# Fewer attention bursts hand part of their exponentials to VectorE: 52 instead of 76, with other scratch space

## The chip, the cores and the metric

The kernel runs on one NeuronCore of a Trainium2 chip. The core has TensorE (PE, matrix products), ScalarE (ACT, activation functions), VectorE (DVE, elementwise work and scans), GpSimd (POOL) and SyncE (SP, which here issues nearly all DMAs). The engines run side by side and wait for each other through semaphores. The metric is the time of one execution on the device in microseconds (us). A difference of 0.2% (1.9 us) is about what a measurement of this kernel can tell from no change.

## The reference

The input x is one sequence of 2048 tokens by 1024 features. Two branches work on it and a gate mixes them:

```
g = sigmoid((x * gate_w).sum(-1))
a = S5(x)          # diagonal complex state-space model, 1024 states
b = MHA(x)         # 32 heads of 32, no mask
out = g * a + (1 - g) * b

# S5:   Bu = x @ B_bar^T ; h_t = Lam_bar * h_(t-1) + Bu_t ; y = 2 Re(C h) + x * Dskip
# MHA:  q,k,v = x @ wqkv ; p = softmax(q k^T / sqrt(32)) ; o = (p v) @ wo
```

The softmax needs 32 x 2048 x 2048 exponentials. They are the largest single piece of work outside TensorE.

## The kernel before, in words

**Bursts.** The 32 heads are worked in 8 groups of four heads (g = 0 to 7), each group in 8 units of 256 queries, each unit in 8 bursts of 256 keys: 512 bursts, numbered B, and p is the same number as a place in time. One burst computes the scores of 4 heads x 256 keys x 256 queries (`burst`, L1651: 8 matmuls on 32 rows each) into two score slots of PSUM out of three, z = 0 and z = 1; a slot holds 128 x 1024 numbers. `exp` (L1658) turns a slot into bf16 weights in SBUF, normally by one ScalarE instruction of 1024 columns per slot (L1667). So a normal burst costs ScalarE two such instructions. `pv` (L1725) later multiplies the weights into V, four small matmuls to a "quarter" and four quarters to a burst; `plan` deals the quarters out over later bursts.

**Shared bursts.** For the bursts in the set `DVB`, `dve_exp` splits slot z = 0: ScalarE does only the first half of it (512 columns, L1692), and VectorE does the other half by integer arithmetic in five instructions: L1693 from PSUM, then L1698 to L1701 (`exp_b` to `exp_f`). I call these bursts shared. They stand at most at every fourth place (B % 4 == 1), so a stretch of four bursts holds one half and seven full exponentials, or eight full ones. The five VectorE instructions need scratch: two result tiles (`xt`), an integer tile (`xi`) and a float tile (`xw`). `x_set` says which of five places a burst uses: the projection weights' buffer `w` of one or the other parity (with the second half of `Ag`), the upper half of the state buffer `hp`, rows 6 and 7 of `OT`, or `ut` and `ub`. Each place belongs to something else at other times, and `x_toks` puts the dependences on whatever writes there next.

**Dense work.** Between the bursts TensorE works off chains of large matmuls ("dense" work), all through PSUM bank 7: projections for the next group (`d_qk` L1422, `d_v` L1440), the state inputs u (`d_u` L1452), the state outputs c (`d_c`: 16 matmuls L1481 and 4 small ones L1487 for the skip term), and at the end the output projection (`d_out` L1512). A chain is 8 large matmuls (c: 16; V: 32 small ones), and VectorE copies its result out of bank 7 before the next chain starts (L1429, L1446, L1458, L1494, L1518). The loop in `build` gives every burst 4 dense matmuls; a shared burst gets 3 and the one before it 5.

**Items.** VectorE also runs the state recurrence: 32 items (4 chunks of 512 steps in time x 8 blocks of 128 states), each two rotations, two scans (L1371) and two rotations back (`item_ops`). The c chains of a chunk may start when its 8 items are done, the u chains of chunks 2 and 3 when the c chains of the chunk that had the state buffer are done.

**The order.** The program is written out in one order per engine at build time. `build` keeps its own estimate of when TensorE, ScalarE and VectorE come free (`self.T`, `self.act_t`, `self.dve_t`) and `fill` places VectorE's background instructions (the rest of a shared exponential first, then items, then preparation) before the next fixed one where the estimate leaves room. SyncE issues weight loads (`ld_w`, L1081), the stores of gated c tiles (L1495), the transposes of finished attention rows (L1751) and output stores, in program order.

Of the kernel before, what the change touches and what calls it, by code (L numbers as in the profile page):

```python
# [942 lines left out]

DVB_FROM = 69
DVB_NOT = (69, 73, 77, 81, 85, 89, 93, 97, 101, 105, 109, 113, 117, 121, 125, 129, 133, 257, 261, 265, 273, 277, 281, 285, 333, 337, 341, 345, 349, 357, 381, 385, 389, 457)


def dve_bursts():
    return [B for B in range(DVB_FROM, 508) if B % 4 == 1 and B not in DVB_NOT]

# [8 lines left out]
class Dense:  # L959

    def __init__(self, pieces, evac, tag):
        self.pieces = pieces
        self.evac = evac
        self.tag = tag
        self.left = sum(w for w, _ in pieces)
        self.after = 0
        self.extra = 0.0
        self.group = None


class FastPath:

    def __init__(self, nc, S, es, d, flag):
# [56 lines left out]

        pair = lambda ap: ap.rearrange("p (h n) -> p h n", h=2)
        half = lambda ap: [pair(ap[:, 0:1024]), pair(ap[:, 1024:2048])]
        hx = [hp[:, r, 4:8, :].rearrange("p a n -> p (a n)") for r in range(2)]
        wx = [self.w[:, x].rearrange("p q a n -> p (q a n)") for x in range(2)]
        ag = self.Ag[:, 1, :]
        self.xt = half(wx[0]) + half(wx[1]) + half(hx[0]) + half(self.OT[:, 6, :]) + [ub[:, 0], ub[:, 1]]
        self.xi = [wx[0][:, 2048:3072], wx[1][:, 2048:3072], hx[1][:, 0:1024], self.OT[:, 7, 0:1024], self.ut[:, 0, :]]
        self.xi = [ap.bitcast(I32) for ap in self.xi]
        self.xw = [ag, ag, hx[1][:, 1024:2048].bitcast(F32), self.OT[:, 7, 1024:2048].bitcast(F32), self.ut[:, 1, :]]
        self.tile += self.xt  # L1040
# [38 lines left out]
    def ld_w(self, g, part, eng="sp"):  # L1079
        cb = 1024 * part + 128 * g  # L1080
        self.dma(lambda e: e.dma_start(self.w[:, g % 2, part], self.wsrc[:, :, cb:cb + 128]), [], [("w", g % 2, part)] + (self.x_toks(g % 2) if g > 2 else []), "ld_w", eng)  # L1081

# [268 lines left out]
    def item_ops(self, j, ch, n):  # L1351
        dve, ub, tq, ut, ht = self.dve, self.ub, self.tq, self.ut, self.ht
        b = self.hp_of[ch]
        hp = self.hpb[b]
        er, ei = self.Et[:, 0, j, :], self.Et[:, 1, j, :]
        k = self.ub_of(n)
        ure, uim = ub[k][:, 0, :], ub[k][:, 1, :]
        u0, u1, Et = ("ub", k, 0), ("ub", k, 1), ("Et", j)
        t = [tq[:, i, :] for i in range(4)]
        ops = []  # L1360

        def tt(c, o, a, b, op, r, w):
            ops.append((c, lambda: dve(lambda e: e.tensor_tensor(o, a, b, op), r, w() if callable(w) else w)))  # L1363
# [12 lines left out]
        tt(0.602, tq[:, 2:4, :], ht[:], E2r, ALU.mult, [("ht", 0), ("ht", 1), Et], [("tq", 2)])  # L1376
        hw = ["warm"] if ch == 0 and j == 0 else []
        late = lambda: []
# [4 lines left out]
        tt(0.335, hp[:, 0, j, :], t[0], t[1], ALU.subtract, [("tq", 0)], lambda: [("hp", b, j, 0)] + hw + late())  # L1383
        tt(0.335, hp[:, 1, j, :], t[2], t[3], ALU.add, [("tq", 2)], lambda: [("hp", b, j, 1)] + hw + late())
        if j == 7 and ch < 3:
            ops.append((0.0, self.carry))
        return ops
# [84 lines left out]
    def d_c(self, ch, tq, cb, k):  # L1472
# [12 lines left out]
        for q in range(4):  # L1485
            dt = 4 * cb + q
            mms.insert(5 * q + 3, (0, lambda e, f, l, q=q, dt=dt: e.matmul(ps[:, 7, 128 * q:128 * (q + 1)], xT[:, dt, 128 * tt:128 * (tt + 1)], self.diagD[:, dt, :],  # L1487
                                                                          start=False, stop=False), [("diagD", dt)] + self.xtok(ch)))
        a = self.Ag[:, 0, :]
        at = ("Ag", 0)  # L1490
        tile = 2 * tt + cb
# [125 lines left out]
    def x_set(self, B):  # L1617

        g, pg = divmod(B, 64)
        if g == 7 or B >= 433:  # L1620
            return 4
        if pg < 52:
            return g % 2
        return 2 if g < 4 else 3

    def x_of(self, B, n):
        return len(self.tile) - 10 + 2 * self.x_set(B) + n

    def x_toks(self, k):
        t0 = len(self.tile) - 10 + 2 * k  # L1630
        assert not any(self.left_in.get(t0 + t, 0) for t in range(2)), (self.p, k)
        assert not self.dx or self.x_now != k
        return [(n, t0 + t) for n in ("pt", "ptd") for t in range(2)] + [("xi", k), ("xw", max(k, 1))]

# [34 lines left out]
    def dve_exp(self, B, s, p):  # L1669
# [22 lines left out]
        self.S.op("act", lambda e: e.activation(t[:, 0, :], ps[:, 2 * s, :], ACT.Exp, scale=SCALE), reads=[("S", s)], writes=[("pt", p)], deps=deps, name="exp")  # L1692
        self.S.op("dve", lambda e: e.tensor_scalar(xi, ps[:, 2 * s + 1, :], EXP_A, EXP_B, ALU.mult, ALU.add), reads=[("S", s)], writes=[("xi", k)], deps=deps, name="exp_a")  # L1693
        kw = max(k, 1)
        I, W = ("xi", k), ("xw", kw)
        assert not self.dx, (self.p, [c for c, _ in self.dx], self.log[-8:])
# [35 lines left out]
    def normalize(self, U):  # L1732
# [23 lines left out]
    def build(self):  # L1756
# [5 lines left out]
        self.holds, self.left_in = {}, {}  # L1762
        self.dx, self.seen_x, self.waiting, self.x_now, self.busy_w = [], set(), set(), None, None
        self.bg2 = []
# [14 lines left out]
        for g in range(1, GROUPS):  # L1779
            for c in range(4):  # L1780
                proj[g][8 + c].after = 16 * c
            for dn in proj[g]:
                dn.group = g
        proj[0] = [self.d_qk(0, 0, 2), self.d_qk(0, 0, 3)]
# [30 lines left out]
        for p in range(first, NBURST):  # L1815
# [35 lines left out]

            if pg == (58 if g else 24) and g + 2 < GROUPS:
                assert g or not (proj[0] or cur and cur.tag == "proj")
                for part in (1, 2, 0):
                    self.ld_w(g + 2, part)
            wsv = self.d["B_wo"].rearrange("(a p) n -> p a n", p=128)
            if p == 437:
                self.dma(lambda e: e.dma_start(self.wo3[0], wsv[:, 0:3, :]), [], ["wo0"] + [("w", 0, q) for q in range(3)] + self.x_toks(0), "ld_wo")
            if not us and cur is None and not wo1 and p > 400:
# [68 lines left out]
            else:  # L1928
                self.fill(self.T + (QK_LAG if p + 1 in DVB else 1.0))
            self.busy_w = cur.group if cur is not None else None  # L1930
            if getattr(self, "seen_items", 0) != self.items_done:
# [31 lines left out]
    def tail(self):  # L1963
# [3 lines left out]
        z = self.ut[:, 1, 0:65]  # L1967
        dve(lambda e: e.memset(z, 0.0), [], ["z"] + [("ut", r) for r in range(2)] + self.x_toks(4))
        assert not self.dx, (self.p, [c for c, _ in self.dx], self.log[-8:])
# [173 lines left out]
```

## Time and profile before

| | |
|---|---|
| median of three runs | 932.32 us (931.59 to 932.56) |
| the profiled execution | 932.32 us, of which 930.6 us is the span from first to last instruction |
| busy in the span | PE 916.7, ACT 914.9, DVE 733.3, POOL 8.9 us |
| granted TensorE clock | 0.996 |
| full exponentials, 128x1024 | 948 on ScalarE |
| half exponentials, 128x512 | 76 on ScalarE, and 76 x 5 instructions on VectorE |

How to read it: busy times overlap, since engines work at once; TensorE's and ScalarE's instructions are also pipelined, so that a ScalarE exponential is recorded as 1.0 to 1.2 us long though the next one starts about 0.9 us after it. Durations of pieces of the program are therefore read from start to start: how long a stretch of bursts took, and what was in it. Bursts 136 to 171 ran at 260.9 to 324.2 us, 188 to 203 at 351.7 to 379.6, 268 to 295 at 491.9 to 542.1 and 352 to 399 at 641.7 to 726.5. The first exponential starts at 9.8 us, and the last burst's at 919.4.

### The profile page before, as it was taken

Reading aid. Unit: us, or ns where it says so; the run is one execution under the profiler, and the core shown is the slowest. Engines: PE = TensorE matmul, PEld = TensorE weight load, DVE = VectorE, ACT = ScalarE, POOL = GpSimd, SP = SyncE. Lnnn points to the kernel's source line nnn. Section 1 sums busy time; section 2 is a strip of 40 time slices with the busy share of each in tenths; the row PEclk is TensorE's granted clock in tenths of the full one; section 3 lists DMA queues with packets and bytes.
Section 4 is the critical chain, followed back from the end, with each engine's and each line's share of the span. In section 5 each row is a group of like instructions: output and inputs, shape, how many; then the busy total and the mean of one; then the engine's idle time right before and its main releaser. Section 6 shows DMA issues by size and latency. Waiting matters only on the chain.

```text
span 930.6 us, 33709 instructions
## 1 busy us (share of the span) xinstructions
PE 916.7 (99%) x15316; PEld 528.4 (57%) x15316; DVE 733.3 (79%) x1349; ACT 914.9 (98%) x1034; POOL 8.9 (1%) x39
## 2 busy tenths in 40 slices
PE   8999999999999999999999999999999999999996
PEld 4555755557555565555655755555655556555553
DVE  2799979999988888886699966579889565766775
ACT  6999999999999999999999999999999999999996
POOL 2000000000000000000000000000000000000000
PEclk9999999999999999999999999999999999999998
DMA  9559433310431004101033201233110212233322
GB/s 204 104 84 154 79 53 76 73 30 5 87 62 42 30 6 86 52 29 31 19 73 63 43 16 56 62 62 72 32 41 8 73 53 93 100 87 123 116 64 75
DMA packets 157076, 60.90 MB, mean 65 GB/s; under 512 B 145664, under 2 KB 145664, under 8 KB 156928
## 3 DMA queue, kind: packets, MB, share of 16 engines
q1 hardware_dynamic: 154768, 58.16, 28.0%
q8 instruction: 121, 1.98, 0.9%
q10 hardware_dynamic: 2160, 0.53, 0.3%
q14 instruction: 27, 0.22, 0.1%
HBM read 16.79 MB, written 12.58 MB: 32 GB/s over the span
## 4 chain that ended last, share of the span: by engine, by line
PE 61%; ACT 36%; DVE 1%; SPq 1%; DMA 1%; issue 0%; DVEq 0%
ACT f_pt L1667 32%; PE f_ps L1725 17%; PE f_ps L1651 13%; PE f_ps L1452 9%; PE f_ps L1481 9%; PE f_ps L1422 8%; PE f_ps L1440 4%; ACT f_ub L1692 1%; SPq L1076 1%; ACT f_wb L1692 1%; DMA f_xT<-in_A_x_dram 1%; ACT f_Et L1667 1%; ACT f_cT_re L1667 1%; PE f_ps L1487 1%; ACT f_cT_im L1667 0%
## 5 line engine op out<-in xcount | busy, mean ns | idle before, releaser
L1667 ACT ACTIVATE f_pt<-f_ps 128x1024 bf16<-128x1024 f32 x868 | 817.7, 1227 | 0.6 <-PE f_ps L1651 0.6
L1725 PEld LDWEIGHTS f_ps<-f_V,f_pt 128*128 128x128 bf16 x6944 | 240.4, 96 | 136.0 <-issue 97.6
L1725 PE MATMUL f_ps<-f_V,f_pt 128*128 128x33 bf16 x6944 | 293.7, 178 | 0.0
L1651 PE MATMUL f_ps<-f_Q,f_K 32*128 32x256 bf16 x4096 | 225.5, 274 | 3.4 <-ACT f_cT_re L1667 1.2
L1651 PEld LDWEIGHTS f_ps<-f_Q,f_K 32*128 32x128 bf16 x4096 | 75.6, 92 | 120.2 <-ACT f_pt L1667 53.5
L1452 PE MATMUL f_ps<-f_xT,f_wb 128*128 128x512 bf16 x512 | 131.0, 377 | 0.9 <-DVE f_pf L1247 0.6
L1422 PE MATMUL f_ps<-f_xT,f_wb 128*128 128x512 bf16 x464 | 119.0, 378 | 0.0
L1371 DVE TENSOR_TENSOR_SCAN f_ht<-f_pf,f_init,f_ut 128x512 bf16<-128x512 f32 x64 | 80.6, 1273 | 0.0
L1481 PE MATMUL f_ps<-f_cT_im,f_hp 128*128 128x512 bf16 x192 | 72.6, 378 | 0.0
L1481 PE MATMUL f_ps<-f_cT_re,f_hp 128*128 128x512 bf16 x192 | 72.5, 378 | 0.0
L1693 DVE TENSOR_SCALAR f_wb<-f_ps 128x512 int32<-128x512 f32 x47 | 32.5, 691 | 49.1 <-PE f_ps L1651 48.7
L1512 PE MATMUL f_ps<-f_wb,f_OT 128*128 128x512 bf16 x252 | 65.9, 380 | 0.0
L1440 PE MATMUL f_ps<-f_wb,f_xT 128*128 128x128 bf16 x896 | 59.1, 219 | 0.0
L1452 PEld LDWEIGHTS f_ps<-f_xT,f_wb 128*128 128x128 bf16 x512 | 40.2, 96 | 32.4 <-issue 0.7
L1422 PEld LDWEIGHTS f_ps<-f_xT,f_wb 128*128 128x128 bf16 x464 | 36.2, 96 | 28.2
L1440 PEld LDWEIGHTS f_ps<-f_wb,f_xT 128*128 128x128 bf16 x896 | 50.4, 97 | 0.1
L1458 DVE CAST f_ub<-f_ps 128x512 bf16<-128x512 f32 x48 | 33.0, 687 | 14.6 <-PE f_ps L1452 14.3
L1363 DVE TENSOR_TENSOR f_tq<-f_ht,f_Et 128x1024 bf16<-128x1024 bf16 x64 | 42.0, 684 | 0.2
L1363 DVE TENSOR_TENSOR f_ut<-f_tq 128x512 f32<-128x512 bf16 x64 | 41.9, 683 | 0.0
L1494 DVE TENSOR_SCALAR f_Ag<-f_ps,f_gcol 128x512 f32<-128x512 f32 x32 | 24.0, 751 | 13.0 <-PE f_ps L1481 12.6
L1700 DVE SCALAR_TENSOR_TENSOR f_Ag<-f_Ag,f_wb 128x512 f32<-128x512 f32 x47 | 32.5, 691 | 1.4
L1692 ACT ACTIVATE f_wb<-f_ps 128x512 bf16<-128x512 f32 x47 | 33.3, 709 | 0.2
(160 smaller groups left out, 937.7 us busy)
## 6 DMA issues: line engine op xcount, KB each, us to landing
ag_scratch<-f_Ag SPq DMA_DIRECT2D x32, 256.0 KB, 2.4
f_hp<-ag_scratch SPq DMA_DIRECT2D x32, 256.0 KB, 3.0
f_wb<-in_B_wqkv_dram SPq DMA_DIRECT2D x21, 256.0 KB, 3.7
out_dram<-f_xT SPq DMA_DIRECT2D x16, 256.0 KB, 2.1
f_wb<-in_B_wo_dram SPq DMA_DIRECT2D x1, 1024.0 KB, 5.3
f_OT<-f_On SPq DMA_TRANSPOSE x63, 2.3
f_wb<-in_B_wo_dram SPq DMA_DIRECT2D x1, 768.0 KB, 6.6
f_wb<-in_B_wqkv_dram ACTq DMA_DIRECT2D x2, 256.0 KB, 4.1
```

What stands on the lines that cost most here:

```text
L1363: ops.append((c, lambda: dve(lambda e: e.tensor_tensor(o, a, b, op), r, w() if callable(w) else w)))
L1371: ops.append((1.192, lambda ri=ri: dve(lambda e: e.tensor_tensor_scan(ht[:, ri, :], rr, ut[:, ri, :], self.init[:, ri, j:j + 1], ALU.mult, ...
L1422: mms.append((1, lambda e, f, l, a=a: e.matmul(ps[:, bank, :], w[:, g % 2, part, a, :], xT[:, a, 512 * ch:512 * (ch + 1)], start=f, stop=l ...
L1440: m = e.matmul(ps[:, bank, 128 * q:128 * (q + 1)], xT[:, a, 128 * kt:128 * (kt + 1)], w[:, g % 2, 2, a, :], start=(a == 0), stop=(a == 7))
L1452: mms.append((1, lambda e, f, l, a=a: e.matmul(ps[:, 7, :], bT[:, n % 2, ri, a, :], xT[:, a, 512 * ch:512 * (ch + 1)], start=f, stop=l), [ ...
L1458: self.dve(lambda e: e.tensor_copy(self.ub[k][:, ri, :], ps[:, 7, :]), [("bank", 7)], [("ub", k, ri)] + over, "evac_u")
L1481: mms.append((1, lambda e, f, l, j=j, ri=ri: e.matmul(ps[:, 7, :], hp[:, ri, j, cols], cT[ri][:, j, 512 * cb:512 * (cb + 1)], start=f, sto ...
L1512: mms.append((1, lambda e, f, l, j=j: e.matmul(ps[:, 7, :], OT[:, j, 256 * qb + 128 * r:256 * qb + 128 * (r + 1)], wo[j][0][:, 512 * cb:51 ...
L1651: m = e.matmul(ps[:, 2 * sl[z] + h % 2, 256 * kl:256 * (kl + 1)], K[32 * h:32 * h + 32, g % 2, 128 * kt:128 * (kt + 1)], Q[32 * h:32 * h + ...
L1667: self.act(lambda e: e.activation(self.tile[p], ps[:, 2 * s:2 * s + 2, :], ACT.Exp, scale=SCALE), [("S", s)], [("pt", p)], "exp")
L1692: self.S.op("act", lambda e: e.activation(t[:, 0, :], ps[:, 2 * s, :], ACT.Exp, scale=SCALE), reads=[("S", s)], writes=[("pt", p)], deps=d ...
L1725: m = e.matmul(ps[:, 6, o:o + 33], self.tile[p][:, h2, 256 * kl + 128 * qt:256 * kl + 128 * (qt + 1)], V[:, g % 2, 2 * i + kl, h, :], star ...
```

## The change

The set of shared bursts becomes smaller. These 24 leave it, none joins it:

137, 141, 145, 149, 153, 157, 161, 165, 169 (nine in a row); 189, 193, 197, 201; 269, 289, 293; 353, 361, 365, 369, 373, 377, 393, 397.

The 52 others stay: 173 to 185, 205 to 253, 297 to 329 and 401 to 505 without 457, each time every fourth. A burst that leaves has two full exponentials on ScalarE and nothing on VectorE, and the dense quota of 4.

The scratch goes from five places to three: the upper half of `hp` up to burst 253, rows 6 and 7 of `OT` up to 391, `ut` and `ub` after that. The weights' buffer `w` and the second half of `Ag` are no longer scratch, so four things that hung on it go back: `d_c` uses both halves of `Ag` in turn, the weights of group g + 2 are loaded at place 24 of group g instead of 58, the first part of the output weights is loaded at p = 386 instead of 437, and `ld_w` has no dependence on scratch. What the remaining scratch overlaps is waited for in other places: the items 4 to 7 of chunk 2 wait for the first set, the transposes of groups 6 and 7 for the second. The rest of the program text is the same: the two wide rotations per state part and the timing model in `build` stand in both.

```diff
-DVB_FROM = 69
-DVB_NOT = (69, 73, 77, 81, 85, 89, 93, 97, 101, 105, 109, 113, 117, 121, 125, 129, 133, 257, 261, 265, 273, 277, 281, 285, 333, 337, 341, 345, 349, 357, 381, 385, 389, 457)
-
-
 def dve_bursts():
-    return [B for B in range(DVB_FROM, 508) if B % 4 == 1 and B not in DVB_NOT]
+    out = []
+    for lo, hi, m in ((172, 188, 4), (204, 254, 4), (296, 332, 4), (400, 508, 4)):
+        out += [B for B in range(lo, hi) if B % m == 1 and B != 457]
+    return out
...
-        self.xt = half(wx[0]) + half(wx[1]) + half(hx[0]) + half(self.OT[:, 6, :]) + [ub[:, 0], ub[:, 1]]
-        self.xi = [wx[0][:, 2048:3072], wx[1][:, 2048:3072], hx[1][:, 0:1024], self.OT[:, 7, 0:1024], self.ut[:, 0, :]]
...
+        self.xt = [hx0[:, 0], hx0[:, 1], row6[:, 0], row6[:, 1], ub[:, 0], ub[:, 1]]
+        self.xi = [hx[1][:, 0:1024].bitcast(I32), row7[:, 0:1024].bitcast(I32), self.ut[:, 0, :].bitcast(I32)]
...
         if ch == 2 and j >= 4:
-            late = lambda: self.x_toks(2)
+            hw = self.x_toks(0)
...
-        a = self.Ag[:, 0, :]
-        at = ("Ag", 0)
+        a = self.Ag[:, k % 2, :]
+        at = ("Ag", k % 2)
...
     def x_set(self, B):
-
-        g, pg = divmod(B, 64)
-        if g == 7 or B >= 433:
-            return 4
-        if pg < 52:
-            return g % 2
-        return 2 if g < 4 else 3
+        return 0 if B < 254 else 1 if B < 392 else 2
...
-        use = (k, B // 64 if k < 2 else 0)
-        self.x_now = k
-        if use not in self.seen_x:
-            self.seen_x.add(use)
+        if not self.seen_x[k]:
+            self.seen_x[k] = True
+            over = [("hp", k, j, ri) for j in range(8) for ri in range(2)]
             if k < 2:
-                assert self.busy_w != B // 64
-                over = [("w", k, q) for q in range(3)] + [("Ag", 1)]
-            elif k < 4:
-                assert self.c_left[k - 2] == 0
-                over = [("hp", k - 2, j, ri) for j in range(8) for ri in range(2)]
+                assert self.c_left[k] == 0
...
         if qb == 0 and g >= 6:
-            assert all(self.x_set(B) != 3 or B < U * BURSTS for B in DVB)
-            x += self.x_toks(3)
+            assert all(self.x_set(B) != 1 or B < U * BURSTS - 8 for B in DVB)
+            x += self.x_toks(1)
...
-            if pg == (58 if g else 24) and g + 2 < GROUPS:
+            if pg == 24 and g + 2 < GROUPS:
...
-            if p == 437:
-                self.dma(lambda e: e.dma_start(self.wo3[0], wsv[:, 0:3, :]), [], ["wo0"] + [("w", 0, q) for q in range(3)] + self.x_toks(0), "ld_wo")
+            if p == 386:
+                self.dma(lambda e: e.dma_start(self.wo3[0], wsv[:, 0:3, :]), [], ["wo0"] + [("w", 0, q) for q in range(3)], "ld_wo")
```

More of the change, by code (lines that the diff above doesn't have):

```diff
@@ L967, in __init__ @@
         self.extra = 0.0
-        self.group = None
 class FastPath:
@@ L1029, in __init__ @@
         self.tile += [self.cT[ri][:, j, :].rearrange("p (h n) -> p h n", h=2) for j in range(8) for ri in range(2)]
-        pair = lambda ap: ap.rearrange("p (h n) -> p h n", h=2)
-        half = lambda ap: [pair(ap[:, 0:1024]), pair(ap[:, 1024:2048])]
+        row6 = self.OT[:, 6, :].rearrange("p (t h n) -> p t h n", t=2, h=2)
+        row7 = self.OT[:, 7, :]
         hx = [hp[:, r, 4:8, :].rearrange("p a n -> p (a n)") for r in range(2)]
-        wx = [self.w[:, x].rearrange("p q a n -> p (q a n)") for x in range(2)]
-        ag = self.Ag[:, 1, :]
-        self.xt = half(wx[0]) + half(wx[1]) + half(hx[0]) + half(self.OT[:, 6, :]) + [ub[:, 0], ub[:, 1]]
-        self.xi = [wx[0][:, 2048:3072], wx[1][:, 2048:3072], hx[1][:, 0:1024], self.OT[:, 7, 0:1024], self.ut[:, 0, :]]
-        self.xi = [ap.bitcast(I32) for ap in self.xi]
-        self.xw = [ag, ag, hx[1][:, 1024:2048].bitcast(F32), self.OT[:, 7, 1024:2048].bitcast(F32), self.ut[:, 1, :]]
+        hx0 = hx[0].rearrange("p (t h n) -> p t h n", t=2, h=2)
+        self.xt = [hx0[:, 0], hx0[:, 1], row6[:, 0], row6[:, 1], ub[:, 0], ub[:, 1]]
+        self.xi = [hx[1][:, 0:1024].bitcast(I32), row7[:, 0:1024].bitcast(I32), self.ut[:, 0, :].bitcast(I32)]
+        self.xw = [hx[1][:, 1024:2048].bitcast(F32), row7[:, 1024:2048].bitcast(F32), self.ut[:, 1, :]]
         self.tile += self.xt
@@ L1080, in ld_w @@
         cb = 1024 * part + 128 * g
-        self.dma(lambda e: e.dma_start(self.w[:, g % 2, part], self.wsrc[:, :, cb:cb + 128]), [], [("w", g % 2, part)] + (self.x_toks(g % 2) if g > 2 else []), "ld_w", eng)
+        self.dma(lambda e: e.dma_start(self.w[:, g % 2, part], self.wsrc[:, :, cb:cb + 128]), [], [("w", g % 2, part)], "ld_w", eng)
     def ld_b(self, j, n):
@@ L1362, in tt @@
         def tt(c, o, a, b, op, r, w):
-            ops.append((c, lambda: dve(lambda e: e.tensor_tensor(o, a, b, op), r, w() if callable(w) else w)))
+            ops.append((c, lambda: dve(lambda e: e.tensor_tensor(o, a, b, op), r, w)))
         E2, E2r = self.Et[:, :, j, :], self.Et[:, ::-1, j, :]
@@ L1377, in item_ops @@
         hw = ["warm"] if ch == 0 and j == 0 else []
-        late = lambda: []
         if ch == 2 and j >= 4:
-            late = lambda: self.x_toks(2)
+            hw = self.x_toks(0)
         if b == 1 and j == 0:
             hw = ["fX", "fY", "m_c"] + self.EFtok + ["gp%d" % i for i in range(4)]
-        tt(0.335, hp[:, 0, j, :], t[0], t[1], ALU.subtract, [("tq", 0)], lambda: [("hp", b, j, 0)] + hw + late())
-        tt(0.335, hp[:, 1, j, :], t[2], t[3], ALU.add, [("tq", 2)], lambda: [("hp", b, j, 1)] + hw + late())
+        tt(0.335, hp[:, 0, j, :], t[0], t[1], ALU.subtract, [("tq", 0)], [("hp", b, j, 0)] + hw)
+        tt(0.335, hp[:, 1, j, :], t[2], t[3], ALU.add, [("tq", 2)], [("hp", b, j, 1)] + hw)
         if j == 7 and ch < 3:
@@ L1617, in x_set @@
     def x_set(self, B):
-        g, pg = divmod(B, 64)
-        if g == 7 or B >= 433:
-            return 4
-        if pg < 52:
-            return g % 2
-        return 2 if g < 4 else 3
+        return 0 if B < 254 else 1 if B < 392 else 2
     def x_of(self, B, n):
-        return len(self.tile) - 10 + 2 * self.x_set(B) + n
+        return len(self.tile) - 6 + 2 * self.x_set(B) + n
     def x_toks(self, k):
[L1630 to L1633, printed above, removed]
+        return [(n, len(self.tile) - 6 + 2 * k + t) for n in ("pt", "ptd") for t in range(2)] + [("xi", k), ("xw", k)]
     def pt_of(self, B, z):
@@ L1693, in dve_exp @@
         self.S.op("dve", lambda e: e.tensor_scalar(xi, ps[:, 2 * s + 1, :], EXP_A, EXP_B, ALU.mult, ALU.add), reads=[("S", s)], writes=[("xi", k)], deps=deps, name="exp_a")
-        kw = max(k, 1)
-        I, W = ("xi", k), ("xw", kw)
+        I, W = ("xi", k), ("xw", k)
         assert not self.dx, (self.p, [c for c, _ in self.dx], self.log[-8:])
@@ L1762, in build @@
         self.holds, self.left_in = {}, {}
-        self.dx, self.seen_x, self.waiting, self.x_now, self.busy_w = [], set(), set(), None, None
+        self.dx, self.seen_x, self.waiting = [], [False] * 3, set()
         self.bg2 = []
@@ L1781, in build @@
                 proj[g][8 + c].after = 16 * c
-            for dn in proj[g]:
-                dn.group = g
         proj[0] = [self.d_qk(0, 0, 2), self.d_qk(0, 0, 3)]
@@ L1929, in build @@
                 self.fill(self.T + (QK_LAG if p + 1 in DVB else 1.0))
-            self.busy_w = cur.group if cur is not None else None
             if getattr(self, "seen_items", 0) != self.items_done:
@@ L1967, in tail @@
         z = self.ut[:, 1, 0:65]
-        dve(lambda e: e.memset(z, 0.0), [], ["z"] + [("ut", r) for r in range(2)] + self.x_toks(4))
+        dve(lambda e: e.memset(z, 0.0), [], ["z"] + [("ut", r) for r in range(2)] + self.x_toks(2))
         assert not self.dx, (self.p, [c for c, _ in self.dx], self.log[-8:])
```

## The prediction

> **What bounds the kernel now.** The page comes first: its busy row and the chain that ended last.
>
> ```profile
> PE 916.7 (99%) x15316; PEld 528.4 (57%) x15316; DVE 733.3 (79%) x1349; ACT 914.9 (98%) x1034; POOL 8.9 (1%) x39
> ...
> PE 61%; ACT 36%; DVE 1%; SPq 1%; DMA 1%; issue 0%; DVEq 0%
> ...
> L1667 ACT ACTIVATE f_pt<-f_ps 128x1024 bf16<-128x1024 f32 x868 | 817.7, 1227 | 0.6 <-PE f_ps L1651 0.6
> ```
>
> TensorE and ScalarE are both busy all the time, and VectorE has a fifth of the span free. The averages can't say which of the two sets the pace in a stretch, so the second view is the busy time of the full exponentials in stretches of bursts. Two of the counted instructions straddle an edge of a window; a burst has two.
>
> ```profile
> core 0: us, ACT busy (x), PEclk, DMA share, GB/s
> 150.90:260.90 110.00, 110.00 (x121) 1.00 0.25 52
> 260.90:324.20 63.30, 60.02 (x65) 1.00 0.18 45
> 351.70:379.60 27.90, 27.13 (x29) 1.00 0.39 82
> 491.90:542.10 50.20, 50.02 (x54) 1.00 0.23 43
> 605.40:641.70 36.30, 36.30 (x42) 1.00 0.37 71
> 641.70:726.50 84.80, 83.94 (x90) 1.00 0.14 29
> ```
>
> The first and the fifth row hold no shared burst: 120 exponentials in 110.0 us are 0.917 us each, 40 in 36.3 us 0.907. ScalarE does them back to back, so eight, one block of four normal bursts, take 7.33 or 7.26 us. That is so whatever dense work TensorE has in them (u, projections, c); here ScalarE is the bound. The second row holds nine shared bursts in 36: 63.3 / 9 = 7.03 us a block.
>
> Third, the timeline of ScalarE, in two places of that row (start, us, then the group):
>
> ```profile
> 283.98 0.60 ACT L1692 ACTIVATE f_wb<-f_ps 128x512 bf16<-128x512 f32 x1
> 284.48 6.59 ACT L1667 ACTIVATE f_pt<-f_ps 128x1024 bf16<-128x1024 f32 x7
> 291.09 0.60 ACT L1692 ACTIVATE f_wb<-f_ps 128x512 bf16<-128x512 f32 x1
> ...
> 312.35 0.60 ACT L1692 ACTIVATE f_wb<-f_ps 128x512 bf16<-128x512 f32 x1
> 312.84 6.52 ACT L1667 ACTIVATE f_pt<-f_ps 128x1024 bf16<-128x1024 f32 x7
> 319.17 0.68 ACT L1692 ACTIVATE f_wb<-f_ps 128x512 bf16<-128x512 f32 x1
> ```
>
> A half exponential holds ScalarE for 0.50 us (283.98 to 284.48), and from half to half a block is 7.11 us in the first place and 6.82 in the second. Seven full ones at 0.907 and one half would be 6.85: the second place is ScalarE's own pace, the first is 0.26 longer. The chain of waits says who is last there:
>
> ```profile
> 287.24 0.40 PE f_ps L1725 x12
> 287.64 0.66 PE f_ps L1481 x3
> 288.30 0.06 PE f_ps L1487
> 288.35 0.22 PE f_ps L1481
> 288.57 0.20 PE f_ps L1725 x8
> 288.76 0.33 PE f_ps L1651 x8
> 289.10 0.40 PE f_ps L1725 x12
> ```
>
> No piece of ScalarE is in it: each step begins where the one before ended. With c chains, which carry the small L1487 as well, TensorE is the bound of a shared block. Where they run is seen in the count of their matmuls (16 fill a block):
>
> ```profile
> core 0: us, PE busy (x) PEld busy (x), PEclk, DMA share, GB/s
> 260.90:324.20 63.30, 25.97 (x96) 7.26 (x96) 1.00 0.18 45
> 379.60:421.90 42.30, 23.77 (x88) 6.69 (x88) 1.00 0.14 44
> 542.10:605.40 63.30, 34.59 (x128) 9.69 (x128) 1.00 0.17 49
> 726.50:775.60 49.10, 30.22 (x112) 8.50 (x112) 1.00 0.20 66
> ```
>
> **What the change costs: the 24 blocks.** Each becomes a block of eight full exponentials. So I price a block, not an instruction, against the profiled execution's 932.32 us, which is also the median of the three runs.
>
> Bursts 136 to 171: 36 bursts at the pace of the unshared stretch just before, 7.33 / 4, are 65.97 us instead of 63.3: +2.67. Bursts 188 to 203: 4 x 7.33 = 29.32 instead of 27.9: +1.42. Bursts 268 to 295: seven blocks, of which I take the unshared pace as 7.30, between 7.26 and 7.33: 51.1 instead of 50.2, +0.9. Bursts 352 to 399: twelve blocks at 7.30 are 87.6 instead of 84.8: +2.8. Sum: +7.8 us, 0.32 a block. The ends: at 7.26 everywhere the four sums are 2.04 + 1.14 + 0.62 + 2.32 = +6.1. The other end is the whole of ScalarE's saving, 0.907 - 0.50 = 0.41 to 0.42 us a burst, +10 us; it is due only if TensorE no longer limits the blocks as they are now, and the 7.11 us blocks exclude it for a third of them.
>
> Here a rule weighs otherwise. The Trainium skill, Perfetto Trace Analysis, section Identifying the Most-Contended Engine, would take the engine of highest occupancy as the bound, and for TensorE the weight-load share instead of the matmul share: ScalarE with 98% against 57%. The skill's ScalarE: Activation LUTs, section What ACT_TABLE_LOAD costs, gives 0.833 ns a column, so as an estimate 0.427 us for the 512 columns that come back (the timeline above: 0.41), and the sum would be 24 x 0.427 = +10.2 us, 942.5. The chain of the 7.11 us blocks, all TensorE, speaks against it.
>
> I keep to the blocks.
>
> **What VectorE gets back.** Its five instructions take 0.691 + 0.452 + 3 x 0.691 = 3.2 us a burst, 77 us in all. None of that is on the chain (DVE 1%), so directly it is worth nothing. Indirectly it lets items, and with them c chains, come earlier. In shared blocks that matters: the kept stretches with c chains run at 42.3 / 6 = 7.05, 63.3 / 9 = 7.03 and 49.1 / 7 = 7.01 us a block, those with other dense work at 6.88 (27.5 / 4 for bursts 172 to 187, where no c matmul is). A block of c that moves from a shared place to an unshared one saves 0.15 us, since unshared blocks cost the same with c as without. The last kept stretch follows the removed eight of 352 to 399, which free 26 us, three or four blocks of VectorE time, for the last items; the three of 268 to 293 free 10 us, one block. For chunk 1 the rule in `build` with 254 in it forces c chains from p = 198 in both programs. I count five blocks of c that move: -0.75 us. Ends: none, and all c matmuls of the kept stretches, (88 + 128 + 112) / 16 = 20.5 blocks, -3.1.
>
> **What is moved.** The second `Ag` half: a c evacuation waits only for TensorE now, as the store of 2.4 us lands long before the next chain of four bursts ends: 0. Weight loads 34 bursts earlier and the output weights 51 bursts earlier: three loads of 256 KB landing in 3.7 us, and one of 768 KB in 6.6 us, each with the readers of the buffer's old content finished (a group's projections end before the group begins) and their own readers at least six bursts, 11 us, later before the change; they stand in SP's queue ahead of the row transposes and c stores, which nothing waits for within a unit. 0, and if that cover went, at most one landing, 6.6 us. POOL's carry instructions keep their place behind the items.
>
> **The waits it adds.** Burst 173's first half exponential waits for the readers of chunk 0's states; if the last c chain were just ahead, ScalarE would stand for one evacuation, 0.75 us. Items 20 to 23 wait, on VectorE, for the products of burst 253; in the profile item 20 comes at about p = 268, so if it came two blocks sooner it would still come after. If not, the copy out of bank 7 behind it and then TensorE would wait, up to about two bursts, 3.6 us. Sets two and three are first used at 297 and 401, and their old content was done with before: c of chunk 1 by p = 232, the items by about p = 392, less the time VectorE gains. I take 0 for all, with +0.75 and +3.6 for the range.
>
> Sum: 932.32 + 7.8 - 0.75 = 939.4 us.
>
> **The rivals.**
>
> *ScalarE's full price (14%).* The blocks' excess over ScalarE's pace moves into the kept blocks or the new unshared ones run slower than 7.33: +10, 942.3 us. For it: unshared bursts 16 to 63 took 89.8 us by ScalarE's timeline, 7.48 a block, with VectorE full of preparation. Against it: VectorE will have less to do.
>
> *The relief is larger (9%).* All unshared pace 7.26 and most c blocks out of shared places: 6.1 - 3.1 = +3, 935.3 us. Against it: chunk 1's place is forced.
>
> *A new wait (4%).* Items 20 to 23 or the scratch handover stop VectorE with a copy out of bank 7 behind it: +11 or so, 943 us.
>
> *No change (2%).* TensorE would be the bound in every block, as its 99% suggests; 932.3 us. Against it are the 7.33 us blocks with the same 16 dense matmuls, which TensorE does in 6.82 when ScalarE lets it.
>
> *Not slower (1%).* One mechanism could give it all back: VectorE's lateness stretches the 52 kept shared blocks, which would go at ScalarE's pace once it has 77 us more. Their rows (42.3 + 48.2 from 421.9 to 470.1, 63.3, 49.1 and the rest at 6.9) average 6.95 against 6.85, so it is worth 52 x 0.10 = -5.2 us. It decides, in favour of no loss, only from 0.15 us a block on, below ScalarE's pace, and the chain in such blocks shows TensorE back to back, not VectorE.
>
> **How the numbers follow.** The forecast has 70%, with 938.0 to 941.0 of its own; it and the rivals on both its sides make slower by over 0.2% 0.97 (70 + 14 + 9 + 4), no change 0.02, faster by over 0.2% 0.01. For 8 in 10 I go to 937.0 (half of the larger relief lies below) and to 942.5, which takes in the full price of ScalarE; the single waits lie above.
>
> **What would show it.** 972 full and 52 half exponentials; the stretch of bursts 136 to 171 at 65.5 to 66.2 us with ScalarE back to back; bursts 352 to 399 at 87 to 88; c matmuls of chunk 3 starting before burst 396; kept stretches with 6.85 to 7.05 us a block; VectorE near 656 us busy. I am wrong if an unshared block costs under 7.2 or over 7.45 us, if kept blocks change by more than 0.1, or if a wait of ScalarE or VectorE at bursts 173, 254 to 264, 297 or 401 exceeds 1 us.

## The result, and the profile after

The changed kernel takes 940.29 us (median; 939.77 to 940.92) against 932.44 us for the kernel before: a ratio of 1.0086, 95% interval 1.0069 to 1.0104. That is +7.85 us; the forecast was +7.1, the time 939.4. The profiled execution took 939.99 us, of which 938.2 us is its span.

The page of the changed kernel (line numbers have moved: L1653 is the full exponential, L1673 the half, L1476 the c matmuls, L1482 the small skip matmuls, L1637 the scores, L1705 the products with V):

```profile
PE 923.3 (98%) x15316; PEld 532.7 (57%) x15316; DVE 659.5 (70%) x1229; ACT 923.0 (98%) x1034; POOL 11.3 (1%) x39
...
PE 60%; ACT 37%; DVE 1%; DMA 1%; issue 0%; DVEq 0%; SPq 0%
...
L1653 ACT ACTIVATE f_pt<-f_ps 128x1024 bf16<-128x1024 f32 x892 | 833.7, 1283 | 0.6 <-PE f_ps L1637 0.6
```

VectorE lost 74 us of work and the kernel became slower: its time is 1% of the chain that ended last, before and after. ScalarE stays at 98%, and its busy time is 8.1 us longer (923.0 after 914.9). The busy time of full exponentials in the stretches of bursts 76 to 135, 136 to 171, 188 to 203, 268 to 295, 332 to 351 and 352 to 399 shows where:

```profile
core 0: us, ACT busy (x), PEclk, DMA share, GB/s
151.10:261.10 110.00, 110.00 (x122) 1.00 0.24 52
261.10:327.10 66.00, 66.00 (x74) 1.00 0.24 55
354.80:384.10 29.30, 29.30 (x34) 1.00 0.22 51
496.10:547.50 51.40, 51.40 (x58) 1.00 0.28 62
610.50:646.80 36.30, 36.30 (x42) 1.00 0.47 93
646.80:734.80 88.00, 88.00 (x98) 1.00 0.13 30
```

The first and fifth rows are as long as before the change. The other four were 63.3, 27.9, 50.2 and 84.8 us and are now 66.0, 29.3, 51.4 and 88.0: +2.7, +1.4, +1.2 and +3.2, together +8.5 us. Full exponentials alone now fill each of them wholly. The timeline of ScalarE around the first burst that stayed shared, 173:

```profile
269.35 60.08 ACT L1653 ACTIVATE f_pt<-f_ps 128x1024 bf16<-128x1024 f32 x65
329.01 0.91 ACT L1673 ACTIVATE f_hp<-f_ps 128x512 bf16<-128x512 f32 x1
329.50 6.83 ACT L1653 ACTIVATE f_pt<-f_ps 128x1024 bf16<-128x1024 f32 x7
335.95 0.87 ACT L1673 ACTIVATE f_hp<-f_ps 128x512 bf16<-128x512 f32 x1
```

65 full exponentials without a gap, and no wait at 173, where the prediction had allowed one. The c matmuls in the four kept stretches that have them:

```profile
core 0: us, PE busy (x) PEld busy (x), PEclk, DMA share, GB/s
261.10:327.10 66.00, 25.90 (x96) 7.54 (x96) 1.00 0.24 55
384.10:426.10 42.00, 25.91 (x96) 7.27 (x96) 1.00 0.23 63
547.50:610.50 63.00, 28.12 (x104) 7.84 (x104) 1.00 0.10 32
734.80:783.90 49.10, 28.07 (x104) 7.86 (x104) 1.00 0.20 66
```

The first row is the removed stretch. In the three others there are 304 where there were 328, so 1.5 blocks of c left them, not five. Over all 52 kept blocks, some of which lie outside these rows, it is 2.0 blocks, 21.5 to 19.5.

Block by block, from start to start, the 24 removed blocks went from 6.986 to 7.326 us on average, +8.17 us; the 52 kept ones gave back 0.40; the rest of the bursts added 0.13.

### The profile page after: what moved, and what is told of

The parts are those of the page before. It is cut to its first block, busy times and chain, and to the rows that moved or that the text cites. A ratio compares the mean times of both kernels' runs of the same rounds, so it can differ in the third digit from the quotient of the medians.

```text
span 938.2 us, 33573 instructions
## 1 busy us (share of the span) xinstructions
PE 923.3 (98%) x15316; PEld 532.7 (57%) x15316; DVE 659.5 (70%) x1229; ACT 923.0 (98%) x1034; POOL 11.3 (1%) x39
## 4 chain that ended last, share of the span: by engine, by line
PE 60%; ACT 37%; DVE 1%; DMA 1%; issue 0%; DVEq 0%; SPq 0%
ACT f_pt L1653 34%; PE f_ps L1705 17%; PE f_ps L1637 13%; PE f_ps L1447 9%; PE f_ps L1476 9%; PE f_ps L1417 8%; PE f_ps L1435 4%; ACT f_ub L1673 1%; DMA f_xT<-in_A_x_dram 1%; ACT f_OT L1653 1%; ACT f_cT_re L1653 1%; ACT f_Et L1653 1%; PE f_ps L1482 1%; ACT f_cT_im L1653 0%; PE f_ps L1142 0%
## 5 line engine op out<-in xcount | busy, mean ns | idle before, releaser
L1653 ACT ACTIVATE f_pt<-f_ps 128x1024 bf16<-128x1024 f32 x892 | 833.7, 1283 | 0.6 <-PE f_ps L1637 0.6
L1705 PEld LDWEIGHTS f_ps<-f_V,f_pt 128*128 128x128 bf16 x7136 | 241.4, 96 | 133.8 <-issue 97.1
L1705 PE MATMUL f_ps<-f_V,f_pt 128*128 128x33 bf16 x7136 | 294.0, 178 | 0.2 <-ACT f_pt L1653 0.2
L1637 PE MATMUL f_ps<-f_Q,f_K 32*128 32x256 bf16 x4096 | 234.2, 273 | 3.8 <-ACT f_pt L1653 1.2
L1637 PEld LDWEIGHTS f_ps<-f_Q,f_K 32*128 32x128 bf16 x4096 | 82.4, 92 | 125.3 <-issue 53.3
L1476 PE MATMUL f_ps<-f_cT_re,f_hp 128*128 128x512 bf16 x192 | 72.5, 378 | 0.2
L1476 PE MATMUL f_ps<-f_cT_im,f_hp 128*128 128x512 bf16 x192 | 72.6, 378 | 0.0
L1417 PEld LDWEIGHTS f_ps<-f_xT,f_wb 128*128 128x128 bf16 x464 | 36.2, 96 | 27.9
L1674 DVE TENSOR_SCALAR f_ut<-f_ps 128x512 int32<-128x512 f32 x26 | 18.0, 692 | 46.7 <-PE f_ps L1637 46.7
L1674 DVE TENSOR_SCALAR f_hp<-f_ps 128x512 int32<-128x512 f32 x17 | 11.8, 691 | 34.4 <-PE f_ps L1637 34.4
L1424 DVE CAST f_Q<-f_ps 128x512 bf16<-128x512 f32 x30 | 20.7, 690 | 17.8 <-PE f_ps L1417 17.8
```

The lines of the kernel that those rows point to most:

```text
L1417: mms.append((1, lambda e, f, l, a=a: e.matmul(ps[:, bank, :], w[:, g % 2, part, a, :], xT[:, a, 512 * ch:512 * (ch + 1)], start=f, stop=l ...
L1476: mms.append((1, lambda e, f, l, j=j, ri=ri: e.matmul(ps[:, 7, :], hp[:, ri, j, cols], cT[ri][:, j, 512 * cb:512 * (cb + 1)], start=f, sto ...
L1637: m = e.matmul(ps[:, 2 * sl[z] + h % 2, 256 * kl:256 * (kl + 1)], K[32 * h:32 * h + 32, g % 2, 128 * kt:128 * (kt + 1)], Q[32 * h:32 * h + ...
L1653: self.act(lambda e: e.activation(self.tile[p], ps[:, 2 * s:2 * s + 2, :], ACT.Exp, scale=SCALE), [("S", s)], [("pt", p)], "exp")
L1705: m = e.matmul(ps[:, 6, o:o + 33], self.tile[p][:, h2, 256 * kl + 128 * qt:256 * kl + 128 * (qt + 1)], V[:, g % 2, 2 * i + kl, h, :], star ...
```

## A better reading of the same records: ends, not starts

The experiments below made me read ScalarE's timeline again. These lines are from the kernel before and continue those in the prediction:

```profile
319.66 6.61 ACT L1667 ACTIVATE f_pt<-f_ps 128x1024 bf16<-128x1024 f32 x7
326.02 0.73 ACT L1692 ACTIVATE f_wb<-f_ps 128x512 bf16<-128x512 f32 x1
326.52 6.66 ACT L1667 ACTIVATE f_pt<-f_ps 128x1024 bf16<-128x1024 f32 x7
332.97 0.70 ACT L1692 ACTIVATE f_wb<-f_ps 128x512 bf16<-128x512 f32 x1
```

From start to start of the halves the three blocks from 312.35 on took 6.82, 6.85 and 6.95 us. But the second number of a line is the recorded length, and that of the half exponentials grows and shrinks: 0.60, 0.68, 0.73, 0.70. From end to end (312.95, 319.85, 326.75, 333.67) the blocks took 6.90, 6.90 and 6.92. A start may run ahead of the engine by a part of an instruction when TensorE is early, and the records lengthen by as much. The ends don't move. Over all exponentials from burst 16 on, the median distance from end to end is 0.917 us up to a full one and 0.490 us up to a half one, in every kernel here. So I add 0.917 per full and 0.490 per half exponential, and call stall what the stretch from burst 15's end to the last exponential's end has above that. In the last column a range of bursts runs from the end of its first exponential to the end of the first one behind the range:

| kernel | shared bursts | ScalarE's work, us | stall, us | stretch, us | stall by bursts: 16-59, 136-171, 204-253, 296-331, 400-441 |
|---|---|---|---|---|---|
| before | 76 | 877.21 | 4.82 | 882.03 | 1.62, 0.85, 0.91, 0.84, 0.66 |
| changed | 52 | 887.46 | 2.62 | 890.08 | 1.63, 0, 0.27, 0.47, 0.38 |

The work rises by 24 x 0.427 = 10.25 us, the whole of ScalarE's price, and the stalls fall by 2.20: 0.85 in bursts 136 to 171, which ScalarE alone now sets, and 1.29 in the kept stretches; the rest is rounding of the two prices. The net is +8.05 us for the stretch. What lies before and after it differs by up to 1 us from run to run of any of these kernels (39.4 to 40.4 us before, 8.1 to 9.2 after), here by -0.5. The stalls stand only where shared blocks hold c chains, and in the opening.

The recorded lengths say more. Here are the half exponentials alone, from the kernel before (bursts 193 to 209), then from the changed kernel (205 to 221); in both the c chains begin just ahead of burst 197:

```profile
360.48 0.81 ACT L1692 ACTIVATE f_wb<-f_ps 128x512 bf16<-128x512 f32 x1
367.36 0.83 ACT L1692 ACTIVATE f_wb<-f_ps 128x512 bf16<-128x512 f32 x1
374.46 0.64 ACT L1692 ACTIVATE f_wb<-f_ps 128x512 bf16<-128x512 f32 x1
381.56 0.60 ACT L1692 ACTIVATE f_wb<-f_ps 128x512 bf16<-128x512 f32 x1
388.67 0.60 ACT L1692 ACTIVATE f_wb<-f_ps 128x512 bf16<-128x512 f32 x1
...
385.99 0.89 ACT L1673 ACTIVATE f_hp<-f_ps 128x512 bf16<-128x512 f32 x1
392.94 0.84 ACT L1673 ACTIVATE f_hp<-f_ps 128x512 bf16<-128x512 f32 x1
399.93 0.76 ACT L1673 ACTIVATE f_hp<-f_ps 128x512 bf16<-128x512 f32 x1
406.95 0.65 ACT L1673 ACTIVATE f_hp<-f_ps 128x512 bf16<-128x512 f32 x1
413.96 0.60 ACT L1673 ACTIVATE f_hp<-f_ps 128x512 bf16<-128x512 f32 x1
```

From end to end the blocks take 6.90, 6.91, 7.06, 7.11 before and 6.90, 6.91, 6.91, 6.96 after. The record shrinks towards 0.60 us, the shortest in either kernel, while the blocks keep ScalarE's 6.91 or so; only at that floor do they become longer. So the length above 0.60 reads as TensorE's lead over ScalarE: a run of shared blocks with c first uses the lead up, over two or three blocks here, and then costs 0.1 to 0.2 us a block. In the changed kernel the full exponentials ahead of burst 205 are recorded at 1.41 us, the longest there are, so the run that starts there has its whole lead.

## The experiments

**Is it the set alone?** The edit:

```diff
-    return [B for B in range(DVB_FROM, 508) if B % 4 == 1 and B not in DVB_NOT]
+    return [B for B in range(DVB_FROM, 508) if B % 4 == 1 and B not in DVB_NOT + (137, 141, ..., 393, 397)]
```

> The kernel before, with only the 24 bursts taken out of the shared set; scratch places, Ag, weight loads and output weights stay as before. Theory (the whole change is the price of 24 blocks): as the changed kernel, +7.8 us, within 1 us of it, and the same block times stretch by stretch. Rival (the scratch and load edits carry part of the result): more than 1.5 us away from the changed kernel.

Measured: 940.57 us, ratio 1.0084 (1.0067 to 1.0101). From end to end the stretch is 890.07 us, against 890.08 in the changed kernel, with the same stalls in the same places to 0.02 us. So the other scratch places, the second half of `Ag` and the earlier loads together are worth nothing that these runs can show, as the prediction had them.

**Do blocks with c cost less?** Two kernels, six bursts each taken out of the set by the same edit.

> The kernel before without the shared bursts 141, 145, 149, 153, 157 and 161, whose blocks hold c chains and took 42.58 us together. Theory (a block goes from TensorE's pace to ScalarE's 7.33 us): 43.98 - 42.58 = +1.4 us. Rival (each burst costs ScalarE's half, 0.41 us): +2.5 us.

Measured: 934.46 us against 932.69, ratio 1.0017 (1.0008 to 1.0027); the six blocks from start to start +1.46 us, the stretch from end to end +1.69.

> The kernel before without the shared bursts 165 to 185, whose blocks hold projections and took 41.27 us together. Theory: 43.98 - 41.27 = +2.7 us, about twice what the six c blocks cost. Rival (each burst costs the same wherever it stands): as for the six c blocks.

Measured: 934.95 us, ratio 1.0024 (1.0014 to 1.0034); the six blocks +2.34 from start to start, the stretch +2.35. The intervals of the two times overlap, so the ends of the profiled executions must carry this: the direction held and the size did not, as the ratio of the stretches is 1.4, not 2. By ends the reason is plain. Both kernels have 6 x 0.427 = 2.56 us more work for ScalarE; the first sheds all 0.87 us of stall in its stretch, the second 0.21 in all, half of it in bursts 204 to 253. My price for projection blocks had counted as cheap what was only a start running ahead.

**What does VectorE's relief bring?** ScalarE takes the slots back while VectorE goes on working:

```diff
+        if B in BACK:
+            self.S.op("act", lambda e: e.activation(t, ps[:, 2 * s:2 * s + 2, :], ACT.Exp, scale=SCALE), reads=[("S", s)], writes=[("pt", p), ("ptd", p)], deps=deps, name="exp")
...
-                    (0.69, lambda: self.dve(lambda e: e.scalar_tensor_tensor(t[:, 1, :], xw, EXP_C0, ev, ALU.add, ALU.mult), [I, W], [("ptd", p)], "exp_f")),
+                    (0.69, lambda: self.dve(lambda e: e.scalar_tensor_tensor(out, xw, EXP_C0, ev, ALU.add, ALU.mult), [I, W], [W] if B in BACK else [("ptd", p)], "exp_f")),
```

> The kernel before; in the 24 bursts ScalarE computes the whole slot, and VectorE still runs five instructions of the same kind on scratch whose result nothing reads, so order, quotas and VectorE's load stay. Theory: the 24 blocks go to 7.33 us, +8.2 us, and the c chains stay where they are, so 940.5 us, 0.4 above the changed kernel's own sum. Rival 1 (ScalarE's full price shows once VectorE isn't relieved): +10, 942.4 us. Rival 2 (the changed kernel won back more by the relief of VectorE): 943 us or more.

Measured: 941.7 us against 932.69, +9.0, ratio 1.0098 (1.0081 to 1.0115). It lies between the theory and its first rival. By ends it is clear: work 887.46, as in the changed kernel, stall 3.70 instead of 2.62. The stall of bursts 136 to 171 is gone here too, while the kept stretches still have 0.71, 0.84 and 0.66, nearly as before the change. So 1.1 us is what the changed order, with c chains in other places and VectorE free, is worth; this run doesn't part the two. The prediction had 0.75 for it.

**Is TensorE the one who is late in shared blocks with c?** Both kernels without the skip term's small matmuls (their output lacks that term):

```diff
-        for q in range(4):
+        for q in range(0):
             dt = 4 * cb + q
             mms.insert(5 * q + 3, ...
```

> The kernel before without the four small matmuls of the skip term x * Dskip in each c chain (so the skip term is missing from the output). Theory (a shared block with c chains goes at TensorE's pace): the 30 such blocks, 7.05 us on average, come down to ScalarE's 6.85, so -6 us; the unshared blocks with c stay at 7.33. Rival (ScalarE or VectorE sets these blocks): within 1 us of the kernel before.

> The changed kernel without the same small matmuls (the skip term is missing from the output). Theory: only 19.5 of its c blocks are shared, so 19.5 x 0.2 = -3.9 us against the changed kernel; the difference to the kernel before without them is then 24 times ScalarE's half, +9.8 us instead of +7.85. Rival (the small matmuls cost the same wherever they stand): both kernels lose the same, and the difference stays +7.9 us.

Measured: 928.0 us (ratio 0.9963, 0.9949 to 0.9977) and 938.22 us (1.0067, 1.0050 to 1.0083), both against the kernel before at 932.09. So -4.1 and, against the changed kernel's 940.29, -2.1; sizes smaller than expected, for a block falls to 6.91 and not to 6.85. From end to end the stretches are 3.4 and 1.2 us shorter, and only this can be put down to the shared blocks; what is left lies before and after, where the runs differ by up to 1 us anyway. The difference of the two kernels is 10.2 us, by times and by stretches: with TensorE out of the way the 24 bursts cost ScalarE's 24 x 0.427. Both stretches have the same stall, 1.42 us, all of it in the opening. The chain of waits in the place that the prediction showed as all TensorE, in the first of these runs:

```profile
282.74 0.92 ACT f_pt L1667
283.65 0.49 ACT f_wb L1692
284.14 6.42 ACT f_pt L1667 x7
290.56 0.49 ACT f_wb L1692
291.05 6.42 ACT f_pt L1667 x7
297.47 0.49 ACT f_wb L1692
```

Now it is all ScalarE, 6.42 / 7 = 0.917 a full one and 0.49 a half. Four small matmuls a chain, each 0.06 us in the chain shown before, were what made TensorE last there. The lead fits: without them no half exponential of the 76 is recorded shorter than 0.76 us.

**Can the skip term leave TensorE and stay in the result?** First by GpSimd, which is idle:

```diff
+        self.pool(lambda e: e.tensor_tensor(x, x, self.Dh[:], ALU.mult), [tok, "Dh"], [tok])
+        self.pool(lambda e: e.tensor_scalar(x, x, self.gcol[:, 0, tt:tt + 1], 0.0, ALU.mult, ALU.add), [tok, "g0"], [tok])
...
-            self.dve(lambda e: e.tensor_scalar(a, ps[:, 7, :], self.gcol[:, 0, tt:tt + 1], None, ALU.mult), [("bank", 7), "g0"], [at], "evac_c")
+            self.dve(lambda e: e.scalar_tensor_tensor(a, ps[:, 7, :], self.gcol[:, 0, tt:tt + 1], self.xn[:, k % 2], ALU.mult, ALU.add), [("bank", 7), "g0", ("xn", k % 2)], [at], "evac_c")
```

> The kernel before with the skip term moved off TensorE: per c tile a load of the 128x512 piece of x, two GpSimd instructions (times Dskip, times gate), and VectorE's evacuation adds the result in the same instruction. Theory: TensorE is relieved as if the small matmuls were gone, so as the run without them, -6 us, 926.6 us. Rival (GpSimd's result comes late, or GpSimd slows VectorE): the evacuation of c waits and holds bank 7, and the time is above 930 us or not better than before.

Measured: 939.46 us, ratio 1.0077 (1.0060 to 1.0093): the rival. The stalls of bursts 296 to 331 and 400 to 441 are gone (0.00 and -0.01), but the opening has 4.5 us instead of 1.6, bursts 60 to 135 1.2, 136 to 171 4.2, 204 to 253 2.0 and 332 to 399 0.5. In the kernel before VectorE is busy for 75% (204 to 253) to 93% (60 to 135) of these five parts, and for 63% and 61% of the two where the stalls went. In the five it became slower, as the timelines of VectorE and GpSimd show around one overlap:

```profile
297.18 0.46 DVE L1710 TENSOR_SCALAR f_wb<-f_wb 128x512 int16<-128x512 int16 x1
297.67 1.52 DVE L1711 SCALAR_TENSOR_TENSOR f_Ag<-f_wb 128x512 f32<-128x512 uint16 x1
```

```profile
297.49 1.15 POOL L1509 TENSOR_TENSOR f_xn<-f_xn,f_Dh 128x512 bf16<-128x512 bf16 x1 [5.84 <-DMA f_xn<-in_A_x_dram]
298.74 1.01 POOL L1510 TENSOR_SCALAR f_xn<-f_xn,f_gcol 128x512 bf16<-128x512 bf16 x1
```

VectorE's instruction, 0.69 us otherwise, was issued while GpSimd's ran, and took 1.52: GpSimd's ended at 298.64, and 0.55 us later VectorE's did. That is so in all 7 places where this instruction and GpSimd's first one overlap: 1.49 to 1.53 us, always ending 0.55 us behind GpSimd's, against 0.69 in the 67 with no GpSimd instruction beside them. The Trainium skill, SBUF — State Buffer, section Who interferes with whom, says that a VectorE instruction with two inputs in SBUF contends with a GpSimd instruction that reads SBUF, and calls the ports that they share an exclusive lock; this overlap agrees. The rival's other half, that GpSimd's result comes late, is not seen: the evacuation (L1492) waited for TensorE alone, 6.0 us in all.

**By VectorE itself, where it has room** (the 16 tiles of chunks 2 and 3):

```diff
+            self.dve(lambda e: e.scalar_tensor_tensor(x, x, self.gcol[:, 0, tt:tt + 1], self.Dh, ALU.mult, ALU.mult), ["xn", "Dh", "g0"], ["xn"], "skip")
+            self.dve_t += 0.75
+        self.later.append((self.p + 3, mult))
```

> The kernel before; for the 16 c tiles of chunks 2 and 3 alone, where VectorE has room, the skip term leaves TensorE: VectorE multiplies the piece of x by Dskip and gate in one more instruction and adds it in the evacuation. Theory (ScalarE's work, 0.917 us a full and 0.490 a half exponential from end to end, plus the stalls of shared c blocks): the stalls of bursts 296 to 331 (0.84 us) and 400 to 441 (0.66 us) go, those of 136 to 253 stay: -1.5 us, 930.8 us. Rival (VectorE becomes late with 0.75 us more per tile): no gain, and stalls elsewhere.

Measured: 935.0 us against 932.75, ratio 1.0021 (1.0012 to 1.0030), slower. The stall of bursts 400 to 441 is gone, but around bursts 232 and 316 single blocks take 8.5 and 10.2 us. Timelines of VectorE and SyncE at the second:

```profile
580.67 0.75 DVE L1517 SCALAR_TENSOR_TENSOR f_diagD<-f_diagD,f_gcol 128x512 bf16<-128x512 bf16 x1 [2.41 <-DMA f_diagD<-in_A_x_dram]
```

```profile
575.11 0.43 SPq L1513 DMA_DIRECT2D f_diagD<-in_A_Dskip_dram  x1
575.58 0.46 SPq L1514 DMA_DIRECT2D f_diagD<-in_A_x_dram  x1
```

The multiplication stood at the head of VectorE's queue until its piece of x had landed, 5 us after its issue, and behind it a shared burst's slot waited. In that run 10 of the 16 multiplications waited, 15.9 us in all. Four had a load of Dskip just ahead, and two of these, the ones above, are what cost the kernel time; the other two waited 2.1 and 1.8 us without a stall of ScalarE. The mended version loads Dskip once, early:

```diff
+        if k == 16:
+            self.dma(lambda e: e.dma_start(self.Dh, self.d["A_Dskip"].unsqueeze(0).to_broadcast([128, 1024])), ...
...
-        self.later.append((self.p + 3, mult))
+        self.later.append((self.p + (12 if k == 16 else 3), mult))
```

> As the earlier run with the skip term of chunks 2 and 3 on VectorE, but Dskip is loaded once, for both halves and long before its first use, and the first multiplication stands twelve bursts after its load. Theory (the two stalls of 1.7 and 3.2 us there were VectorE waiting for these loads at the head of its queue): they go, and -1.5 us against the kernel before remains, 931.2 us. Rival (the extra 0.75 us per tile makes VectorE late by itself): stalls elsewhere, no gain.

Measured: 931.05 us against 932.04, ratio 0.9989 (0.9980 to 0.9998). From end to end the stretch is 880.58 us instead of 882.03: the stalls of the two stretches are at -0.01, and the 1.45 us is what remains. This is a gain below the 0.2% that a comparison of times resolves well; the ends carry it.

> The same with burst 457 shared as well, 77 shared bursts. Theory: one half exponential less on ScalarE, 0.427 us off the run before it, -1.9 us against the kernel before, unless the double evacuations of the output chains there hold it up. Rival: no gain from 457, as TensorE or VectorE sets bursts 456 to 459.

Measured: 930.61 us, ratio 0.9986 (0.9977 to 0.9995), the lowest median here of a kernel with the whole result, though not clear of the run before it. The one shared burst more took 0.43 us from ScalarE's work (876.78 after 877.21), but the stretch is 880.57, the same, with 0.41 us of stall in bursts 296 to 331 that the run before didn't have. Whether 457 pays is not settled by this.

**Still more shared bursts,** three in eight from 457 on, on top of the first version on VectorE. The edit lets the rest of a shared burst be flushed before the next one; from burst 455 on `plan` may also deal out 4 instead of 3 quarters beside a shared burst:

```diff
+            while p in DVB and self.dx:
+                self.dve_t += self.dx[0][0]
+                self.dx.pop(0)[1]()
             second = self.burst(p)
```

> As the run before it, and from burst 457 on three shared bursts in eight (places 1, 4 and 6) instead of two without 457: 19 instead of 12. Theory: each takes 0.427 us off ScalarE: -1.5 - 7 x 0.427 = -4.5 us, 927.9 us. Rival (VectorE can't do a shared burst every 2 to 3 bursts beside the output evacuations, TensorE waits for bank 7 or for late weights): stalls of 2 us and more after burst 457, and little or no gain.

> The same with places 1, 3 and 6. Theory: the same -4.5 us. Rival (spacing matters, as VectorE takes 3.2 us for a shared burst and two bursts last 3.2 us): up to 1 us worse than with places 1, 4 and 6.

Measured: 941.94 us (ratio 1.0098, 1.0084 to 1.0111) and 947.08 us (1.0148, 1.0134 to 1.0162). Besides the two stalls of their base, bursts 442 and on have 10.4 and 15.6 us of stall, where the kernel before has none. The waits of the first, from burst 457 on:

```profile
PEld f_ps L1672 <- DVE f_ut L1714: 7.1, 12, 1.3
PEld f_ps L1672 <- ACT f_pt L1688: 6.8, 16, 0.6
ACT f_pt L1688 <- PE f_ps L1672: 6.7, 18, 1.1
```

TensorE waits for a score slot that VectorE hasn't read (L1672 is the scores, L1714 VectorE's first instruction of a shared burst, L1688 the full exponential), and ScalarE then for TensorE. So VectorE comes last here, with 3.2 us for a shared burst every 2 or 3 bursts beside its evacuations. It isn't full, though: from 832 to 925 us, which holds these bursts, it is busy for 79.9 of 93.0 us. The spacing of two bursts is the worse, by 5 us, more than the 1 us expected. What the flush and the quarters cost by themselves I did not run. I read it as VectorE's queue at each place, and not its time in all, that limits the number of shared bursts.

## Why the prediction was right

- *The 24 blocks, +7.8.* Measured +8.17 from start to start. Blocks became 7.326 us, the 7.33 of the stretch just before; the 7.30 taken for two stretches was a little low. The mis-sized term is ScalarE's own pace: 0.907 and 6.85 us a block, read from starts, are 0.917 and 6.91 by ends. The sum still came out, since pricing a block from the rows counts work and stall together.
- *ScalarE's full price as the upper end, +10.* It is the actual increase of work, 10.25; what kept the kernel from it are 2.2 us of stalls that went away. The statement that TensorE limits the shared blocks with c was right but for the first blocks of a run, and the pair without the small matmuls shows it. The rule that the prediction cited from the Trainium skill, Perfetto Trace Analysis, section Identifying the Most-Contended Engine, to take ScalarE as the bound by its 98%, gives 10.2, which is what these two runs differ by; it missed in the kernels as they are by those 2.2 us. The 0.427 us that follow from the Trainium skill, ScalarE: Activation LUTs, section What ACT_TABLE_LOAD costs, as an estimate of 512 columns at 0.833 ns agree with the measured 0.917 - 0.490.
- *C chains that move, -0.75.* In start-to-start blocks -0.40, by ends -1.29, and 1.1 by the run in which VectorE wasn't relieved. Two blocks of c moved and not five, and all c matmuls of the kept blocks were 21.5 blocks, not 20.5; chunk 3's c began at burst 392 and not 396, chunk 2's at 288 and not 296. That the size came near is luck, for 0.15 us a block was not the right unit: the first shared blocks of a run with c cost nothing and the later ones 0.1 to 0.2 us. So a stall falls also where c stays: in bursts 204 to 253 from 0.91 to 0.27, with 104 c matmuls after 96, as the run of shared blocks begins there with TensorE's whole lead.
- *Waits added, 0.* The profile has no wait of ScalarE between 261 us and the end of the bursts (the stalls above are too small for it and show only in the ends), and the blocks of bursts 173, 253, 297 and 401 have none by ends either. VectorE's waits in that part, up to 760 us, are for TensorE but for 0.2 us.
- *What was moved, 0.* Shown by the run with the set alone.
- *What was to show it.* Bursts 136 to 171 took 66.0 us and 352 to 399 88.0, as stated. Kept blocks were to change by no more than 0.1, and here the prediction missed: from start to start six of 52 changed by more, -0.17 to +0.15, and by ends those of 205, 209, 309 and 317, by -0.11 to -0.22, where a stall went away. VectorE's 659.5 us are 3 more than stated.

## What to carry to other kernels

Where two engines are both busy all the time, price a change by whole blocks of the schedule, taken from stretches of the same trace that already look as the changed ones will; the price of the instruction alone (10.2 us) is off by the waits that come or go with it. For the pace of a pipelined engine take the distance from end to end, since starts can run ahead by what the recorded length then grows. Where records lengthen as the engine ahead gains a lead, their length is a gauge: a stall comes only when the lead is used up. And an engine that is idle on average (VectorE, busy 79%) is no reserve at a given place: its queue is in order, and one instruction there that waits for a load stops what stands behind it.

## What the runs showed that I had not expected

- ScalarE's cost is 0.917 us for 1024 and 0.490 us for 512 columns back to back, 0.834 ns a column and 63 ns an instruction, by the median of every kernel here to 0.001 us; the recorded lengths of the same full exponentials go from 1.02 to 1.42 us.
- Four 128x128 matmuls of 0.06 us in a chain of sixteen of 0.22 us decide which engine is last: without them the kernel took 4.1 us less of 932, 3.4 of it in the stretch from end to end.
- GpSimd's 128x512 multiplication of 1.15 us holds up a VectorE instruction with two SBUF inputs: in 7 of 7 overlaps it ended 0.55 us behind GpSimd's, after 1.49 to 1.53 us instead of 0.69.
